# One of the last four row moves of a first DFT given to ScalarE, and a negative mean factor made in one GpSimd step

## The chip, the core and the metric

The kernel runs on one core of a Trainium2 chip. TensorE multiplies matrices, VectorE and ScalarE do elementwise work, GpSimd does elementwise work and issues transfers, SyncE only issues transfers. A transfer (DMA) is carried out by the core's 16 DMA engines, whichever engine issued it. The metric is the device time of one execution in microseconds (us); lower is better. Below, PE is TensorE, DVE is VectorE, ACT is ScalarE, POOL is GpSimd, SP is SyncE, as in the profile.

## The reference, cut to what matters

```python
h = layernorm(x) * (1 + ca) + sa            # x: 4096 rows of 640
X = rfft2(h)                                # over the 4096 rows (the other axis has length 1)
z = X.reshape(..., 4 blocks, 160)
hr, hi = relu2(z @ w1 + b1)                 # complex, block-diagonal
o = softshrink(h @ w2 + b2, 0.01)
x = x + ga * irfft2(o)
h = layernorm(x) * (1 + cb) + sb
x = x + gb * ((silu(h @ w_gate) * (h @ w_up)) @ w_down)
```

`sa, ca, ga, sb, cb, gb` come from `silu(c) @ w_mod`. All of it is float32. The change touches only the first line and the way its result gets into the first part of the transform.

## The kernel before, in words

The 4096 rows are seen as 128 times 32: partition p of a tile holds row p of each of 32 groups, and eight tiles `xa0` to `xa7` hold four groups each (128 partitions by 4 by 640). The first stage handles the eight tiles one after another. For a tile t, `ln_stats(t)` takes mean and variance of each row on DVE (L193, L195) and makes from them, on POOL, the factor `rs` = (variance + eps) to the power -0.5 (L197, L198) and `nm` = -mean * `rs` (L407, L408). `ln_apply(t)` normalises the rows in place: the first rows of a tile on ACT (L419, which needs `rs` and `nm`), the others on DVE (L417, which needs mean and `rs`). How many rows ACT takes is a short table, (4, 2, 2, 3, 2, 3, 2, 1) for the eight tiles. In the first two tiles the statistics are made row by row, in the others four rows at a time. `dft_a(t)` is the first DFT, 128 points over the partitions, on PE (L440), and `evac_a(t)` copies its result from PSUM back into the same tile (L450 on DVE, L452 and L454 on ACT).

The second DFT (`stage_b`, L617) needs the same numbers in another layout: a tile `g` per chunk of frequencies. `moves(t)` brings them there. Most go by way of the DRAM scratch `s1` (`write_s1`, L356, then `load_g`, L312). For chunk 0, which PE wants first, the rows of the tiles 6 and 7 go straight from SBUF to SBUF: `move_g(0, t, i, queue)` (L317) copies the rows of one group i, 16 pieces of 2560 bytes, 40 KB. Each tile has four such moves. In tile 7, i = 0 is issued by POOL and i = 1, 2, 3 by SP, in that order, and PE's first L617 needs all of them. The end of tile 7's evacuation is: i = 0 on ACT, i = 1 on DVE, three weight copies on ACT (L284), i = 2 on ACT (L454), the last columns of all four groups on ACT (L452), i = 3 on DVE (L450).

Behind the moves of tile 7 the queue of SP holds the second half of the weights `w2` (`rr`, L498), more writes of `s1`, and the loads of chunk 1. Behind the last evacuation ACT makes the rounded parts of the weights `w1` and `w2` (L284, L538) and copies a bias (L493), then the first result of the second DFT (`z`, L624). While chunk 0 is on its way PE has matmuls `pz` (L335, 16 passes in the profile) whose result nobody reads.

Everything here is inside `tc.manual_schedule()`: each engine runs its instructions in the order in which the program states them for it. Completion of transfers is counted by eight counters, `DMAHW0` to `DMAHW7`, for those issued by SP and ACT together (POOL has its own). The builder hands the counters out in turn, one transfer after another in its own list; each finished transfer adds 16. A transfer that gets a counter waits first until the transfers that had the counter before it have finished, unless its engine has already waited for that. The waits of an instruction are shown below in brackets.

Of the kernel before, what the change touches and what calls it, by code (L numbers as in the profile page):

```python
# [9 lines left out]
OP = mybir.AluOpType  # L10
# [163 lines left out]
def body(tc, x, w1, b1, w2, b2, wg, wu, wd, c, wm, k_fa, k_tb, k_tx, k_bm, k_bx, k_ga, k_ge, k_id, out, dbg=None):  # L174
    nc = tc.nc
    pe, act, dve, pool = nc.tensor, nc.scalar, nc.vector, nc.gpsimd
# [10 lines left out]
    def layer_stats(pl, src, n, name):  # L187

        st = pl.tile([P, n, 2, 6], F32, tag="st", bufs=3, name=f"st_{name}")
        mv = pl.tile([P, n, 2], F32, tag="mv", bufs=7, name=f"mv_{name}")  # L190
        for i in range(n):
            for h in range(2):
                dve.bn_stats(st[:, i, h, :], src[:, i, h * 320:(h + 1) * 320])  # L193
        for i in range(n):
            dve.bn_aggr(mv[:, i, :], st[:, i, :, :])  # L195
        rs = pl.tile([P, n], F32, tag="rs", bufs=7, name=f"rs_{name}")
        pool.tensor_scalar(rs, mv[:, :, 1], EPS, None, op0=OP.add)  # L197
        pool.tensor_tensor(rs, rs, mhalf[:, :n], op=OP.pow)  # L198
        return mv, rs

    from contextlib import ExitStack
    with ExitStack() as top:
# [9 lines left out]
        mone = per.tile([P, 8], F32, name="mone")  # L212
# [26 lines left out]
        with ExitStack() as af:  # L239
# [11 lines left out]
            def load_weights(pl, w, nm, parts=(0, 1)):  # L251
                raw = [pl.tile([P, 2, NB, BS], F32, tag=tag, name=f"{tag}{nm}") for tag in ("rm", "rr")]
                for i in parts:
                    nc.sync.dma_start(raw[i], w[i])
                return raw
# [41 lines left out]
            def load_tb(ch):  # L297
                tb = lp.tile([P, 4, 128], F32, tag="tb", bufs=2, name=f"tb{ch}")
                nc.sync.dma_start(tb, k_tb[:, 4 * ch:4 * ch + 4])
                tbs[ch] = tb  # L300


            def load_g(ch, us=None):
                if ch not in gs:
                    gs[ch] = fx.tile([P, 4, D], F32, tag="gx", bufs=2, name=f"g{ch}")
                f, e = (ch, 1) if ch < 2 else (2, 2) if ch < 4 else (3, 4)
                src = s1[f].rearrange("(u v) (q e j) d -> e u (v q) (j d)", u=4, e=e, q=4)[ch % e]
                if us is None:
                    nc.sync.dma_start(gs[ch].rearrange("p j d -> p (j d)"), src.rearrange("u r d -> r u d"))
                else:  # L310
                    for u in us:
                        nc.sync.dma_start(gs[ch][u:P:4].rearrange("p j d -> p (j d)"), src[u])  # L312


            def move_g(ch, t, i, dma):
                p = 64 * (t % 2) + 16 * i + t // 2
                dma.dma_start(gs[ch][p:p + 13:4], xas[t][64 * ch:64 * ch + 64:4, i])  # L317
# [23 lines left out]
            with tc.tile_pool(name="sp", bufs=1) as sp:  # L341
# [3 lines left out]
                def load_x(t):  # L345
                    xa = xts[t]
                    if t < 3:
                        for i in range(4):
                            nc.sync.dma_start(xa[:, i, :], xv[:, 4 * t + i, :])
                    else:  # L350
                        nc.sync.dma_start(xa, xv[:, 4 * t:4 * t + 4, :])
                    xas.append(xa)


                def write_s1(t, f):
                    nc.sync.dma_start(s1[f][4 * t:4 * t + 4].rearrange("n r d -> r n d"),  # L356
                                      xas[t][(slice(0, 64, 4), slice(64, P, 4), slice(2, P, 4), slice(1, P, 2))[f]])
# [9 lines left out]
                def moves(t):  # L367
                    if t < 6:
                        write_s1(t, 0)
                    if t < 4:  # L370
                        write_s1(t, 1)
                    if t == 0:
                        load_x(6)
                        nc.sync.dma_start(c5, c)
                    elif t == 1:
                        load_x(7)
                        raws[1] = load_weights(sp, w1, "1")
                    elif t == 2:
                        nc.sync.dma_start(wm1, wm[:, 1])
                    elif t == 3:  # L380
                        load_tb(0)
                        pool.dma_start(b1m, b1[:, 0:8].rearrange("p (r b) -> p r b", r=2))
                        pool.dma_start(b1r, b1[0:64, 8:12])
                        pool.dma_start(b2s[0:1], b2.rearrange("r b o -> (r b o)").unsqueeze(0))
                    elif t == 4:

                        raws[2] = load_weights(rp, w2, "2", (0,))
                        load_g(0, (0, 1))
                    elif t == 5:
                        for f in (2, 3):  # L390
                            write_s1(1, f)
                    elif t == 6:

                        for i in range(4):
                            move_g(0, t, i, (pool, nc.sync)[i // 2])
                        load_g(0, (2,))
                    elif t == 7:
                        for i in range(4):
                            move_g(0, t, i, nc.sync if i else pool)


                def ln_stats(t):
                    n = 1 if t < 2 else 4
                    for i in range(0, 4, n):
                        mv, rs = layer_stats(lp, xas[t][:, i:i + n, :], n, f"a{t}_{i}")
                        nm = lp.tile([P, 4], F32, tag="nm", bufs=7, name=f"nm{t}_{i}")
                        pool.tensor_tensor(nm[:, :n], mv[:, :, 0], rs, op=OP.mult)  # L407
                        pool.tensor_tensor(nm[:, :n], nm[:, :n], mone[:, :n], op=OP.mult)  # L408
                        for k in range(n):
                            stats[t, i + k] = (mv[:, k, 0:1], rs[:, k:k + 1], nm[:, k:k + 1])  # L410

                def ln_apply(t):
                    xa = xas[t]
                    for i in range(4):
                        mean, rs, nm = stats[t, i]
                        if i >= (4, 2, 2, 3, 2, 3, 2, 1)[t]:
                            dve.tensor_scalar(xa[:, i, :], xa[:, i, :], mean, rs, op0=OP.subtract, op1=OP.mult)  # L417
                        else:
                            act.activation(xa[:, i, :], xa[:, i, :], AF.Identity, bias=nm, scale=rs)  # L419
# [23 lines left out]
                def evac_a(t):  # L443
                    xa = xas[t]
                    for i in range(5):
# [7 lines left out]
                        else:  # L453
                            act.activation(xa[:, i, 0:512], pas[t, i], AF.Copy)  # L454

                ln_stats(0)
                ln_stats(1)
                ln_apply(0)
                for t in range(8):
                    if t + 2 < 8:  # L460
                        ln_stats(t + 2)
                    if t + 1 < 8:
                        ln_apply(t + 1)
                    dft_a(t)
                    if t == 6:

                        prep1 = prep_weights(raws[1], w1a, w1b, w1c, True)
                        for job in prep1[:3]:
                            weights_high(*job, pool)
                        first_scale(0, 2)  # L470
                    evac_a(t)
                    if t == 6:
                        first_scale(2, 4)
                    if t == 5:
                        act.activation(sc, c5, AF.Silu)
                    moves(t)
# [625 lines left out]
        with ExitStack() as ff:  # L1102
# [1395 lines left out]
            mv, rs, _ = fst[3]  # L2498
# [103 lines left out]
```

## Time and profile before

| what | value |
|---|---|
| three runs | 1406.67, 1402.82, 1402.7 us; median 1402.82 us |
| the profiled execution | 1405.31 us, of which 1403.5 us are the span that the profile shows |
| PE, DVE, ACT, POOL busy | 98%, 76%, 54%, 43% of the span |
| 40 to 50 us: PE, DVE, ACT, POOL busy | 10.00, 9.38, 8.66, 7.78 us |
| 50 to 54 us: the same | 3.44, 3.90, 3.60, 0.00 us |
| DMA engines, mean busy share, 40 to 50 and 50 to 54 us | 0.94 and 0.71 |
| clock granted to TensorE | 1.00 |

The profiled execution is 2.5 us above the median of the runs, so times inside it are added up against its own 1405.31 us and the difference is carried to the median. A row of the timeline gives start, duration, engine, line, what is written and read, and in brackets how long the engine stood idle before it and what released it; rows with "q" behind the engine's name (SPq, ACTq) are transfers being issued, and their duration is that of the issuing, not of the transfer. The chain of waits goes back from the last instruction to what released it, step by step.

### The profile page before, as it was taken

What the parts mean: (1) busy time and instruction counts of PE and PEld (TensorE: products, weight loads), DVE (VectorE), ACT (ScalarE), POOL (GpSimd) and SP (SyncE); (2) the same over time, 40 slices, a digit from 0 to 9 for tenths busy, and PEclk for the clock granted to TensorE, in tenths of its full rate; (3) what the DMA queues carried; (4) which work ended last, traced back from release to release, by engine and by line L of the source; (5) the groups of instructions that cost most, each with busy time, mean ns of one, the idle gap of its engine ahead of it and who ended that gap; (6) DMA issues with size and microseconds to landing.
All of it is one profiled execution on the core that took longest, in us unless ns stands there. A gap on an engine that the chain in (4) does not pass through costs nothing.

```text
span 1403.5 us, 23813 instructions
## 1 busy us (share of the span) xinstructions
PE 1382.4 (98%) x8418; PEld 1310.8 (93%) x8418; DVE 1063.4 (76%) x1868; ACT 763.5 (54%) x1550; POOL 606.6 (43%) x709
## 2 busy tenths in 40 slices
PE   7999999999999999999999999999999999999998
PEld 2799999968889899899999999999999999999998
DVE  8989888889987888649777767677588757375644
ACT  6889999755554555446455355536163624262341
POOL 5610200167776594335446434547153624042240
PEclk9999999999999999999999999999999999999999
DMA  9975566665998998898867998697998668956534
GB/s 371 335 259 186 184 191 220 202 193 177 324 351 303 338 322 273 314 357 303 314 219 288 379 331 300 220 330 238 372 321 300 230 201 287 349 191 222 196 116 150
DMA packets 170858, 377.34 MB, mean 269 GB/s; under 512 B 22028, under 2 KB 81484, under 8 KB 168724
## 3 DMA queue, kind: packets, MB, share of 16 engines
q1 hardware_dynamic: 161588, 359.31, 74.0%
q0 software_dynamic: 6848, 13.90, 3.1%
q10 hardware_dynamic: 2304, 2.62, 0.5%
q8 instruction: 66, 1.08, 0.3%
q14 instruction: 52, 0.43, 0.1%
HBM read 269.48 MB, written 96.80 MB: 261 GB/s over the span
## 4 chain that ended last, share of the span: by engine, by line
PE 83%; DVE 7%; DMA 4%; POOL 2%; issue 2%; ACT 1%; SPq 0%; ACTq 0%; DVEq 0%; POOLq 0%
PE pw L2112 9%; PE pw L2114 9%; PE pw L2113 9%; PE pc L2414 8%; PE pe L2414 6%; PE pd L2330 6%; PE pc L738 5%; PE pl L681 4%; PE pg L2037 3%; PE pg L2035 3%; PE pg L2036 3%; PE pw L2125 2%; PE pw L2123 2%; PE pw L2124 2%; PE pb L617 2%
## 5 line engine op out<-in xcount | busy, mean ns | idle before, releaser
L1499 DVE TENSOR_TENSOR wb<-r,wb 128x768 fp32r<-128x768 f32 (+3 forms) x170 | 161.0, 957 | 14.3 <-ACT wb L1492 13.9
L2112 PE MATMUL pw<-h,wt 128*128 128x384 f32 x412 | 139.6, 339 | 1.0 <-DMA wt<-td 1.0
L2114 PE MATMUL pw<-h,wt 128*128 128x384 f32 x412 | 138.3, 336 | 0.0
L2113 PE MATMUL pw<-h,wt 128*128 128x384 f32 x412 | 138.1, 335 | 0.0
L1492 ACT ACTIVATE wb<-r 128x768 fp32r<-128x768 f32 (+3 forms) x168 | 104.5, 638 | 54.4 <-PE pw L2125 41.2
L2414 PE MATMUL pc<-wq,L 128*128 128x320 f32 x846 | 132.7, 309 | 0.0
L2173 POOL TENSOR_TENSOR sg<-s_x,sg 128x384 f32<-128x384 f32 x24 | 29.1, 1213 | 234.2 <-DVE s_x L2139 234.2
L2414 PEld LDWEIGHTS pc<-wq,L 128*128 128x128 f32 x846 | 126.3, 188 | 0.0
L2193 DVE TENSOR_TENSOR L<-sg,L 128x384 fp32r<-128x384 f32 x144 | 100.2, 718 | 29.8 <-ACT L L2189 29.3
L2131 ACT ACTIVATE s_x<-pw 128x384 f32<-128x384 f32 x52 | 25.5, 491 | 166.4 <-PE pw L2114 165.8
L2112 PE MATMUL pw<-h,wb 128*128 128x384 f32 x312 | 105.0, 336 | 1.5 <-DVE x L2371 1.5
L2113 PE MATMUL pw<-h,wb 128*128 128x384 f32 x312 | 104.4, 335 | 0.0
L2114 PE MATMUL pw<-h,wb 128*128 128x384 f32 x312 | 104.4, 334 | 0.0
L2414 PE MATMUL pe<-wq,L 128*128 128x320 f32 x648 | 101.8, 309 | 0.4 <-DMA wq<-wqd 0.4
L2035 PE MATMUL pg<-ht,wb 128*128 128x512 f32 x260 | 101.9, 392 | 0.0
L2037 PE MATMUL pg<-ht,wb 128*128 128x512 f32 x260 | 101.4, 390 | 0.1
L2036 PE MATMUL pg<-ht,wb 128*128 128x512 f32 x260 | 101.3, 390 | 0.0
L2184 POOL TENSOR_TENSOR sg<-sg,sg 128x384 f32<-128x384 f32 x72 | 92.5, 1285 | 19.5 <-DVE L L2193 16.0
L2414 PEld LDWEIGHTS pe<-wq,L 128*128 128x128 f32 x648 | 96.5, 188 | 0.7 <-issue 0.7
L2330 PE MATMUL pd<-wq,a 128*128 128x320 f32 x632 | 96.8, 310 | 0.0
L2330 PEld LDWEIGHTS pd<-wq,a 128*128 128x128 f32 x632 | 93.5, 188 | 0.5
L2371 DVE TENSOR_TENSOR x<-x,pe 128x320 f32<-128x320 f32 x108 | 51.7, 483 | 51.1 <-PE pe L2457 31.6
(323 smaller groups left out, 3888.1 us busy)
## 6 DMA issues: line engine op xcount, KB each, us to landing
wq<-wqd SPq DMA_DIRECT2D x83, 640.0 KB, 5.7
wt<-td SPq DMA_DIRECT2D x103, 512.0 KB, 4.5
hs<-ho SPq DMA_DIRECT2D x52, 512.0 KB, 5.8
h<-hs SPq DMA_DIRECT2D x32, 768.0 KB, 8.3
td<-wt SPq DMA_DIRECT2D x25, 512.0 KB, 7.0
r<-in_B_w_gate_dram SPq DMA_DIRECT2D x24, 384.0 KB, 4.6
r<-in_B_w_up_dram SPq DMA_DIRECT2D x24, 384.0 KB, 3.7
xx<-tt SPq DMA_DIRECT2D x56, 160.0 KB, 3.2
```

What stands on the lines that cost most here:

```text
L1492: def high(ks, e=slice(0, c), copy=lambda o, i: act.activation(o, i, AF.Copy)):
L1499: dve.tensor_tensor(wbs[t, n][:, 1, ks, e], raw[t, n][:, ks, e], f32(wbs[t, n][:, 0, ks, e]), op=OP.subtract)
L2035: mm(b, wh, hh, start=(kk == 0), stop=False)
L2036: mm(b, wh, hl, start=False, stop=False)
L2037: mm(b, wl, hh, start=False, stop=(kk == 4))
L2112: mm(b, w(0, kp), a[:, kp, 0], start=start and kp == 0, stop=False, skip_group_check=not start)
L2113: mm(b, w(0, kp), a[:, kp, 1], start=False, stop=False, skip_group_check=not start)
L2114: mm(b, w(1, kp), a[:, kp, 0], start=False, stop=kp == 1, skip_group_check=not start)
L2184: pool.tensor_tensor(o, x, y, op=op)
L2193: dve.tensor_tensor(o[:, 1], raws[j], f32(o[:, 0]), op=OP.subtract)
L2330: mm(b[:, :320], l, m, start=start and i == 0, stop=stop and i == len(s) - 1)
L2414: mm(o[:, :320], ls[q][:, x, k], w[:, q, y], start=start and q == 0 and n == 0, stop=q == 1 and n == 2, skip_group_check=not start)
```

## The change

Two edits in the first stage. In `moves(7)` the group i = 2 is issued by ACT (`nc.scalar`) instead of SP; i = 0 stays on POOL, i = 1 and 3 on SP. In `ln_stats`, for the tiles 0 and 1 (one row at a time), `nm` is made by one POOL instruction with two multiplications, and only for the rows that ACT normalises; for two rows of tile 1, which DVE normalises, it isn't made at all. The other tiles keep their two steps.

```diff
@@ moves @@
                     elif t == 7:
                         for i in range(4):
-                            move_g(0, t, i, nc.sync if i else pool)
+                            move_g(0, t, i, (pool, nc.sync, nc.scalar, nc.sync)[i])
+                ACT_ROWS = (4, 2, 2, 3, 2, 3, 2, 1)
@@ ln_stats @@
-                        pool.tensor_tensor(nm[:, :n], mv[:, :, 0], rs, op=OP.mult)
-                        pool.tensor_tensor(nm[:, :n], nm[:, :n], mone[:, :n], op=OP.mult)
+                        if n > 1:
+                            pool.tensor_tensor(nm[:, :n], mv[:, :, 0], rs, op=OP.mult)
+                            pool.tensor_tensor(nm[:, :n], nm[:, :n], mone[:, :n], op=OP.mult)
+                        elif i < ACT_ROWS[t]:
+                            pool.tensor_scalar(nm[:, 0:1], mv[:, 0, 0:1], rs, -1.0, op0=OP.mult, op1=OP.mult)
@@ ln_apply @@
-                        if i >= (4, 2, 2, 3, 2, 3, 2, 1)[t]:
+                        if i >= ACT_ROWS[t]:
```

On PE, DVE and SP the instructions keep their order, but for the one move that leaves SP; POOL has ten instructions less. The new line numbers are five higher behind the edits.

The first place is SP's queue from the second write of tile 3 (`xa_118`) to the moves of tile 6 (`xa_122`). Here `xa_116` is tile 1, `xa_120` tile 4, `xa_121` tile 5, `s` the scratch, `tb` the table of the second DFT, `rm` and `rr` weights. Before:

```order
L356 DMA s<-xa_118 16x4x640 [waits DMAHW5_49]
L299 DMA tb_408<-in_k_tb_dram 128x512 [waits DMAHW6_49]
L356 DMA s<-xa_120 16x4x640 [waits DMAHW7_49,DVE_49,Activation_49]
L254 DMA rm_453<-in_A_w_dram 128x1280 [waits DMAHW0_49]
L312 DMA g_456<-s 32x2560 [waits DMAHW1_49]
L312 DMA g_456<-s 32x2560 [waits DMAHW4_49,DMAHW2_49]
L356 DMA s<-xa_121 16x4x640 [waits DMAHW3_49,DVE_49,Activation_49]
L356 DMA s<-xa_116 32x4x640
L356 DMA s<-xa_116 64x4x640 [waits DMAHW5_49]
L317 DMA g_456<-xa_122 4x4x640 [waits DMAHW6_49,Activation_49]
L317 DMA g_456<-xa_122 4x4x640 [waits DMAHW7_49,DVE_49]
```

The same place in the changed kernel:

```order
L356 DMA s<-xa_118 16x4x640 [waits DMAHW5_49]
L299 DMA tb_398<-in_k_tb_dram 128x512 [waits DMAHW7_49]
L356 DMA s<-xa_120 16x4x640 [waits DMAHW0_49,DVE_49,Activation_49]
L254 DMA rm_443<-in_A_w_dram 128x1280 [waits DMAHW1_49]
L312 DMA g_446<-s 32x2560 [waits DMAHW2_49]
L312 DMA g_446<-s 32x2560 [waits DMAHW4_49,DMAHW3_49]
L356 DMA s<-xa_121 16x4x640 [waits DVE_49,Activation_49]
L356 DMA s<-xa_116 32x4x640 [waits DMAHW5_49]
L356 DMA s<-xa_116 64x4x640 [waits DMAHW6_49]
L317 DMA g_446<-xa_122 4x4x640 [waits DMAHW7_49,Activation_49]
L317 DMA g_446<-xa_122 4x4x640 [waits DMAHW0_49,DVE_49]
```

No transfer has moved here, but the counters have: `tb` had counter 6 and now has 7, and all behind it are one further on. Counter 6 at that turn has gone to ACT's move, which the builder's list puts between `xa_118` and `tb`. So the holder of counter 6 ahead of the write of tile 1 (`xa_116`, 64x4x640) is now ACT's move of tile 7, and the built program makes that write wait for counter 6 to reach 64: 48 from the three transfers that had it earlier, and 16 from ACT's move.

The second place is SP's queue right behind it, from the load of the third quarter of `g` to the weights `rr`; `xa_123` is tile 7. Before:

```order
L312 DMA g_456<-s 32x2560 [waits DMAHW3_49,DMAHW0_49]
L317 DMA g_456<-xa_123 4x4x640 [waits DMAHW1_49,DVE_49,Activation_49]
L317 DMA g_456<-xa_123 4x4x640 [waits DMAHW2_49]
L317 DMA g_456<-xa_123 4x4x640 [waits DVE_49]
L498 DMA rr_454<-in_A_w_dram 128x1280 [waits DMAHW4_49]
```

And in the changed kernel:

```order
L312 DMA g_446<-s 32x2560 [waits DMAHW4_49,DMAHW1_49]
L317 DMA g_446<-xa_123 4x4x640 [waits DMAHW2_49,DVE_49,Activation_49]
L317 DMA g_446<-xa_123 4x4x640 [waits DMAHW3_49,DVE_49]
L503 DMA rr_444<-in_A_w_dram 128x1280
L356 DMA s<-xa_117 32x4x640 [waits DMAHW5_49]
```

One move of tile 7 has left; with `rr` the counters are in step again.

The third place is ACT behind the last evacuation of tile 7, in the changed kernel:

```order
L459 ACTIVATE xa_123<-pa_2_529 128x512 [waits DVE_49,PE_49]
L457 ACTIVATE xa_123<-pa_4_523 128x4x128 [waits PE_49]
L317 DMA g_446<-xa_123 4x4x640 [waits Activation_49]
L284 ACTIVATE w1a<-rm_311 128x4x128
L284 ACTIVATE w1b<-rm_311 128x4x128
L284 ACTIVATE w1c<-rr_312 128x4x128
```

Before, L284 followed L452 directly; now the move stands between, and waits for ACT's own last evacuation.

## The prediction

> **What bounds the kernel now.** I read the page's chain of waits by engine, then the chain in order of time around the two edited places, then the timelines of PE, SP, ACT and POOL there.
>
> ```profile
> PE 83%; DVE 7%; DMA 4%; POOL 2%; issue 2%; ACT 1%; SPq 0%; ACTq 0%; DVEq 0%; POOLq 0%
> ...
> 38.26 0.33 DVE mv_a L195 x4
> ...
> 49.64 3.39 DMA g<-xa
> 53.03 0.35 issue
> 53.38 2.04 PE pb L617 x16
> ```
>
> Over the whole span PE sets the end. In the first stage it doesn't: from 8.5 to 40 us the chain is DVE's statistics, piece on piece, and then one transfer, a move of tile 7 that SP issues at 49.64 and that lands 3.39 us later, at 53.03. PE starts the second DFT 0.35 us behind it. What PE does around that and afterwards:
>
> ```profile
> 52.10 0.72 PE L335 MATMUL pz<-ones 128*128 128x128 f32 x5
> 53.38 0.57 PE L617 MATMUL pb<-tb,g 128*128 128x128 f32 x3 [0.56 <-DMA g<-xa]
> 54.00:60.00 6.00, 6.00 (x54) 6.00 (x53) 5.09 (x13) 4.83 (x11) 3.77 (x7) 1.00 0.99 303
> 100.00:200.00 100.00, 99.94 (x782) 99.03 (x781) 89.16 (x173) 95.03 (x196) 13.69 (x48) 1.00 0.58 185
> ```
>
> PE stands still for 0.56 us at 53.38 and is then busy without a gap (6.00 of 6.00, 99.94 of 100). So whatever moves the 53.38 moves the end by as much, unless PE's later waits give some back.
>
> **The moves as they are issued.** SP's queue, one row for each issue:
>
> ```profile
> 43.96 0.60 SPq L356 DMA_DIRECT2D s<-xa  x1
> 45.12 0.69 SPq L317 DMA_DIRECT2D g<-xa  x1
> 45.91 1.12 SPq L317 DMA_DIRECT2D g<-xa  x1
> 47.13 0.53 SPq L312 DMA_DIRECT2D g<-s  x1
> 48.43 0.56 SPq L317 DMA_DIRECT2D g<-xa  x1
> 49.04 0.54 SPq L317 DMA_DIRECT2D g<-xa  x1
> 49.64 0.54 SPq L317 DMA_DIRECT2D g<-xa  x1
> 50.22 0.45 SPq L498 DMA_DIRECT2D rr<-in_A_w_dram  x1
> ```
>
> The first is the 640 KB write of tile 1 (64x4x640), then two moves of tile 6, the load of the third quarter of g, the three moves of tile 7, and rr. Read alone, the edit takes out the middle move (49.04) and lets the last one go 0.60 us sooner. But the counters say something else. In the changed kernel the 640 KB write waits for counter 6 at 64, and the last 16 of it come from ACT's move. That move can't be issued before ACT's last evacuation:
>
> ```profile
> 47.81 0.60 ACT L452 ACTIVATE xa<-pa 128x512 f32<-128x512 f32 x1 [0.26 <-PE pa L440]
> 280.43 0.44 ACT L853 ACTIVATE cz<-pi 128x320 f32<-128x320 f32 x1 [0.70 <-PE pi L852]
> 280.89 0.35 ACTq L854 DMA_DIRECT2D s<-cz  x1
> 281.29 0.44 ACT L853 ACTIVATE cz<-pi 128x320 f32<-128x320 f32 x1 [0.42 <-PE pi L797]
> ```
>
> So SP, which now issues the write at 43.96, will stand in front of it until a transfer has landed that starts after 48.41 (47.81 + 0.60). Queued behind the waiting write are both moves of tile 6, the load of g, two moves of tile 7, rr, and all later writes and loads. PE's first L617 needs the five of them that go to g. They are late next.
>
> **Costing it.** That SP really stands still for a landing is seen in the waits of SP's queue; the durations of transfers are in the DMA views (KB each, median us from issue to landing; for the moves, the minimum, median and maximum over all eight).
>
> ```profile
> SPq L312 <- DMA s<-xa: 3.2, 4, 2.2
> ...
> s<-cz ACTq DMA_DIRECT2D x4, 160.0 KB, 1.8
> ...
> s<-xa SPq DMA_DIRECT2D x1, 640.0 KB, 5.4
> ...
> DMA to landing us min/median/max: 3.3/3.9/4.1
> ```
>
> 1. ACT's move is issued at 48.44, by the 0.02 us between the end of L853 (280.43 + 0.44) and the issue at 280.89. An issue of its shape took SP 0.54 to 0.56, the 160 KB on ACT 0.35.
> 2. It lands 1.8 us later (ACT's own transfers, on a quiet queue) or up to 3.9 (median of the moves, with other traffic). By then SP has issued nothing since the write before, at 43.3, and the queues have drained. I take 2.0: landing at 50.45.
> 3. SP wakes. PE's wake-up above was 0.35; I take 0.2: 50.65.
> 4. Six issues in a row, the write, two moves, the load, two moves. All they wait for is long done. The starts of the last five lie 0.60 + 0.56 + 0.56 + 0.53 + 0.56 and five gaps of 0.05 (48.43 + 0.56 to 49.04) behind: 50.65 + 3.06 = 53.7 for the last move. The two long issues before (0.69, 1.12) had older transfers ahead; if they come back, 0.7 more.
> 5. Landing of the last move: 1.8 us if nothing is ahead, 3.39 as now, 4.1 as the slowest. The write of 640 KB, the load and four moves are ahead as before, nothing older is: 2.8, nearer to 3.39. That is 56.5.
> 6. PE starts 0.35 later, at 56.85 instead of 53.38: **+3.5 us**.
>
> With the low ends (1.8, 1.8) it is 53.5 + 1.8 + 0.35 = 55.65, +2.3; with the high ends (3.9, the stalls, 4.1) 56.3 + 4.1 + 0.35 = 60.75, +7.4. The values near the low end are likelier, as the queue is quiet.
>
> *The skill on the wait.* The Trainium skill (DMA: Bandwidth & Descriptors, "Why a DMA increments its semaphore by 16 and not by 1") says that a transfer on k of 16 engines posts 16 - k at once and the rest as each engine's data lands, and that only the full 16 means landed. By that the 64 can't be reached at the issue. If it could, SP would go on at 49.0 and PE at 55.2, +1.8. No row here shows the counter; the 3.2 us of SP's waits for landings agree.
>
> **ACT's side.** The move costs ACT 0.4 to 0.6 us ahead of its weight copies. What covers it:
>
> ```profile
> 53.04 0.56 ACT L538 ACTIVATE w2b<-rm 128x160 fp32r<-128x160 f32 x2
> 54.55 0.69 ACT L624 ACTIVATE z<-pb,ca 128x512 fp32r<-128x512 f32 x1 [0.95 <-PE pb L617]
> ```
>
> ACT has 0.95 us of idle ahead of z, and z itself comes 3.5 later. The last w2b copies reuse tile 1's buffer and wait, before and after, for the 640 KB write; issued at 50.65 and landing after 5.4 at most, that is 56.05, plus 0.56, while z is due at 58.0. Hidden: 0. Without that cover it would be 0.6. rr goes out at 54.3 instead of 50.22, 4.1 later against PE's 3.5, with less ahead of it than its old place had; 0 to 0.6, I take 0.
>
> **POOL's part.** Timeline of the first rows and of the turn to four rows at a time:
>
> ```profile
> 6.54 0.19 POOL L407 TENSOR_TENSOR nm<-mv_a,rs_a 128x1 f32<-128x1 f32 x1
> 6.81 0.19 POOL L408 TENSOR_TENSOR nm<-nm,mone 128x1 f32<-128x1 f32 x1
> 7.07 0.22 POOL L197 TENSOR_SCALAR rs_a<-mv_a 128x1 f32<-128x1 f32 x1
> 17.66 12.06 PE L440 MATMUL pa<-xa,fa 128*128 128x512 f32 x26 [1.58 <-DVE xa L417]
> 17.29 0.41 POOL L197 TENSOR_SCALAR rs_a<-mv_a 128x4 f32<-128x4 f32 x1 [0.60 <-DVE mv_a L195]
> 19.63 1.73 ACT L419 ACTIVATE xa<-xa,nm,rs_a 128x640 f32<-128x640 f32 x2 [2.30 <-POOL nm L408]
> ```
>
> A step less is 0.27 us (6.54 to 6.81), in six rows; two rows lose 0.53 (6.54 to 7.07): 2.7 us of POOL in all. The new instruction isn't in the trace: 0.19 as a product, 0.22 as L197; even at 0.46 it would cost no more than the two it replaces. ACT's rows start up to a microsecond sooner. But PE then waits for DVE (1.58), POOL for DVE (0.60), and ACT for the four rows of the next tile (2.30), all set by DVE's statistics, which don't wait for POOL. The gain ends there: 0. Without that cover, with POOL as the bound to the end of the stage, it would be 2.7.
>
> Sum: 3.5 + 0 + 0. The profiled execution would go from 1405.31 to 1408.8; the runs' median is 2.5 lower, so **1402.8 becomes 1406.3 us**, +0.25%, within the 0.3% (4.2 us) that a measurement of this kernel can tell from no change.
>
> **The rivals.**
>
> *A, PE starts slow again after the gap.* PE would stand from 52.82 (52.10 + 0.72) to 56.85, 4.0 us. The groups of L440 matmuls from 8 to 11 us and from 12 to 15 us:
>
> ```profile
> L440 PE MATMUL pa<-xa,fa 128*128 128x512 f32 x4 | 3.5, 1032 | 8.0 <-ACT xa L419 8.0
> ...
> L440 PE MATMUL pa<-xa,fa 128*128 128x512 f32 x8 | 3.9, 618 | 0.0
> ```
>
> After 8.0 us of idle the first four took 1032 ns each instead of 618; after the 1.58 us at 17.66 the 26 went at 464 ns each (12.06 / 26), at full pace. 4.0 lies between. Price: four times 0.41, 1.7 us, as PE is without a gap behind it: +5.2, 1408.0, slower by 0.37%. Against it: the granted clock reads 1.00 in every stretch, and 4.0 is nearer to 1.58 than to 8.0. It decides as soon as the gap is long enough.
>
> *The skill on this.* The Trainium skill (TensorE: Matmul & The Clock Gate, Part 1: The HAM clock gate) has the array fall to half clock after an idle window of about 3.4 us, in windows that run freely. By that a gap of 4.0 us is cold where it covers a whole window, which it does in some executions only: (4.0 - 3.4) / 3.4, an estimate of one in six. The slow matmuls at 8 us agree.
>
> *B, the counter is slow.* ACT's move lands at 3.9, or the moves behind the 640 KB at 4.1 with the long issues: +5 to +7.4, say 1408.8. For it: the moves' row. Against it: the drained queues.
>
> *C, the wait doesn't bite* (counter 6 reaches 64 otherwise, or early). Then the last move goes 0.60 sooner, and PE can't start before 52.82: at best -0.56, 1402.3. With the early opening, +1.8. Against it: the wait stands in the built program, and nothing else adds to that counter in between.
>
> *D, PE's later waits give some back.* The longest from 300 us on:
>
> ```profile
> PE pw L2112 <- DVE x L2371: 1.5, 1, 1.5
> PE pw L2112 <- DMA wt<-td: 1.0, 1, 1.0
> ```
>
> Only loads that SP issues far ahead could use the time: the 1.0, and a few tenths elsewhere. +2.3, 1405.1.
>
> **How the numbers follow.** Forecast (+2.6 to +4.2 around 3.5) 0.52; A 0.16, as the gap is nearer to the one that cost nothing; B 0.14; C 0.08; D 0.10. A and B are slower by more than 0.3%, and so is a twentieth at the forecast's upper edge: 0.32. C holds what chance there is of faster, 0.02. The rest, 0.66, is within 0.3%. The likeliest gives 1406.3, by itself 1405.4 to 1407.0. The range takes in D and the early opening of C below and A and most of B above: 1403.6 to 1409.0.
>
> **What would show it.** Right: SP issues nothing between 43.9 and about 50.5, then six transfers in three microseconds; PE's wait for a landing before L617 grows from 0.56 to about 4; the DMA engines idle around 49 us; DVE's chain ends at 38.6 as before; ACT's first L419 starts 0.2 sooner. Wrong: SP issues the 640 KB write near 44 (then C); L617's first three matmuls take clearly longer than the 0.57 us of now while the gap is about 4 (A); the 53.38 moves by over 5 us (B); the 53.38 moves by 3.5 and the end by less (D).

## The result and the profile after

The changed kernel takes 1411.5 us (median of 6, 1410.68 to 1413.38) against 1404.15 us of the kernel before (median of 6, 1402.7 to 1406.67). The ratio is 1.0051, with a 95% interval of 1.0041 to 1.0062: 7 us slower, twice what was forecast. Five later runs of it gave 1410.2 us, ratio 1.0043 [1.0031, 1.0055]. The profiled execution has a span of 1410.0 us (before: 1403.5).

SP's queue in the changed kernel (start, duration of the issuing; rows of one kind are drawn together):

```profile
41.24 0.48 SPq L312 DMA_DIRECT2D g<-s  x1
41.94 9.38 SPq L356 DMA_DIRECT2D s<-xa  x3
51.42 1.68 SPq L317 DMA_DIRECT2D g<-xa  x2
```

Three writes that were issued one behind the other before now lie across 9.38 us. The stretch from the third of them on, by itself:

```profile
50.73 0.60 SPq L356 DMA_DIRECT2D s<-xa  x1
51.42 1.68 SPq L317 DMA_DIRECT2D g<-xa  x2
53.20 0.53 SPq L312 DMA_DIRECT2D g<-s  x1
53.82 1.19 SPq L317 DMA_DIRECT2D g<-xa  x2
55.06 0.44 SPq L503 DMA_DIRECT2D rr<-in_A_w_dram  x1
```

The 640 KB write goes out at 50.73 instead of 43.96, and all the rest of the queue stands behind it. ACT at that time:

```profile
47.62 0.60 ACT L457 ACTIVATE xa<-pa 128x512 f32<-128x512 f32 x1 [0.26 <-PE pa L445]
48.24 1.15 ACTq L317 DMA_DIRECT2D g<-xa  x1
...
60.76 0.69 ACT L629 ACTIVATE z<-pb,ca 128x512 fp32r<-128x512 f32 x1 [5.92 <-PE pb L622]
```

ACT issues its move at 48.24, as soon as the last evacuation is through, and SP goes on 2.49 us later. `z` waits 5.92 us for PE, so ACT's own extra work costs nothing. The chain of waits there:

```profile
54.48 3.85 DMA g<-xa
58.33 0.35 issue
58.67 4.74 PE pb L622 x24
```

The last move of tile 7, issued at 54.48, lands 3.85 later. PE begins the second DFT at 58.67, 5.29 later than before (53.38). And the first 24 matmuls take 4.74 us. In the timeline of PE, with the gap ahead of them, and in the windows from 54 to 60 and 60 to 70 us (the last three columns are granted clock, DMA share and GB/s):

```profile
58.67 4.74 PE L622 MATMUL pb<-tb,g 128*128 128x128 f32 x24 [6.05 <-DMA g<-xa]
```

```profile
54.00:60.00 6.00, 1.33 (x6) 1.36 (x7) 0.69 (x4) 0.83 (x4) 0.00 (x0) 0.64 0.83 235
60.00:70.00 10.00, 10.00 (x77) 9.86 (x76) 6.96 (x14) 7.69 (x17) 8.14 (x16) 0.88 0.90 315
```

In the kernel before the row of the same 24 read, at a granted clock of 1.00,

```profile
53.38 2.92 PE L617 MATMUL pb<-tb,g 128*128 128x128 f32 x24 [0.56 <-DMA g<-xa]
```

Now PE has stood for 6.05 us, the clock in that window is 0.64, and 1.82 us more are gone. From matmul to matmul the first 18 start 0.213 us apart, the others 0.111. So PE is about 7.1 us late behind them (5.29 + 1.82).

### The profile page after: what moved, and what is told of

The parts are those of the page before. It is cut to its first block, busy times and chain, and to the rows that moved or that the text cites. A ratio compares the mean times of both kernels' runs of the same rounds, so it can differ in the third digit from the quotient of the medians.

```text
span 1410.0 us, 23805 instructions
## 1 busy us (share of the span) xinstructions
PE 1383.7 (98%) x8418; PEld 1312.7 (93%) x8418; DVE 1063.0 (75%) x1868; ACT 764.6 (54%) x1550; POOL 611.6 (43%) x699
## 4 chain that ended last, share of the span: by engine, by line
PE 85%; DVE 7%; DMA 3%; POOL 2%; ACT 1%; issue 1%; SPq 0%; ACTq 0%; POOLq 0%; DVEq 0%
PE pw L2117 9%; PE pw L2119 9%; PE pw L2118 9%; PE pc L2419 8%; PE pe L2419 6%; PE pc L743 5%; PE pd L2335 4%; PE pl L686 4%; PE pg L2040 3%; PE pg L2042 3%; PE pg L2041 3%; PE pb L622 3%; PE pw L2130 2%; PE pw L2128 2%; PE pw L2129 2%; PE py L1753 1%
## 5 line engine op out<-in xcount | busy, mean ns | idle before, releaser
L1504 DVE TENSOR_TENSOR wb<-r,wb 128x768 fp32r<-128x768 f32 (+3 forms) x170 | 154.7, 920 | 15.7 <-ACT wb L1497 15.4
```

The costliest lines, as they stand in the source:

```text
L1504: dve.tensor_tensor(wbs[t, n][:, 1, ks, e], raw[t, n][:, ks, e], f32(wbs[t, n][:, 0, ks, e]), op=OP.subtract)
```

## The experiments

All times are medians; the kernel before is run beside each.

**Which of the two edits.** First GpSimd's part alone:

```diff
-                            move_g(0, t, i, (pool, nc.sync, nc.scalar, nc.sync)[i])
+                            move_g(0, t, i, nc.sync if i else pool)
```

> Only the GpSimd part of the change: nm in one step for tiles 0 and 1, all three later moves of tile 7 on SP as before. Counter theory (the loss is SP waiting for ScalarE's move): no difference from the kernel before, ratio 0.999 to 1.001, and L617 starts between 53.1 and 53.5 us. Rival (the earlier ScalarE rows and DVE/GpSimd port traffic cost something): 1 to 3 us slower.

1405.18 us, ratio 1.0004 [0.9994, 1.0013]. PE's timeline of this run:

```profile
53.28 2.92 PE L622 MATMUL pb<-tb,g 128*128 128x128 f32 x24
```

The second DFT begins where it did. GpSimd's saved steps don't help, and the new instruction does no harm. Then the move alone, on the kernel before:

```diff
-                            move_g(0, t, i, nc.sync if i else pool)
+                            move_g(0, t, i, (pool, nc.sync, nc.scalar, nc.sync)[i])
```

> Only the move: i = 2 of tile 7 on ScalarE, nm as before. Counter theory: the whole loss, 6.5 to 7.5 us over the kernel before, SP silent from about 43.9 to 50.7, L617 at 58.5 to 59. Rival (both parts needed): clearly less than 6 us.

1411.36 us, ratio 1.0053 [1.0036, 1.007]. SP's queue, then PE:

```profile
42.54 8.85 SPq L356 DMA_DIRECT2D s<-xa  x3
```

```profile
59.17 5.03 PE L617 MATMUL pb<-tb,g 128*128 128x128 f32 x24 [6.46 <-DMA g<-xa]
```

The whole loss belongs to the move.

**Is it the counter, or that ACT carries the row?** All moves stay on SP, as before. ACT issues one more transfer of the same rows at the same place, into a scratch in DRAM that nobody reads:

```diff
+    spare = nc.dram_tensor("spare", (16, D), F32, kind="Internal").ap()
...
+                            if i == 2:
+                                nc.scalar.dma_start(spare, xas[t][0:64:4, i])
```

> The kernel before with all three moves on SP as before, and one more transfer on ScalarE at the same place: the same 16 rows of 2560 bytes, written to a DRAM scratch that nobody reads. It adds 40 KB of work and takes nothing from SP. Counter theory: it takes counter 6 too, SP waits for it in front of the 640 KB write, and the loss is that of the change or 0.6 us more, as SP has seven issues behind the wait instead of six: 7 to 9 us. Rival (the row of g comes late because ScalarE carries it, by a slow queue or late issue): PE doesn't need this transfer, so 0 to 0.6 us.

1410.83 us, ratio 1.0049 [1.0033, 1.0066]. SP's queue, ACT, and PE's first matmuls of the second DFT:

```profile
42.76 8.47 SPq L357 DMA_DIRECT2D s<-xa  x3
...
53.72 1.75 SPq L318 DMA_DIRECT2D g<-xa  x3
```

```profile
48.76 0.58 ACTq L402 DMA_DIRECT2D spare<-xa  x1
```

```profile
59.21 5.46 PE L620 MATMUL pb<-tb,g 128*128 128x128 f32 x24 [6.06 <-DMA g<-xa]
```

Nobody needs ACT's data here, and SP stands as long. What is shared is the counter: by the semaphore events of the trace ACT's transfer lands at 50.61 on the counter for which SP's 640 KB write waits, and the write is issued at 50.63. The rival, that the row comes late because ACT carries it, falls.

**The same move from GpSimd**, whose transfers have counters of their own:

```diff
-                            move_g(0, t, i, (pool, nc.sync, nc.scalar, nc.sync)[i])
+                            move_g(0, t, i, (pool, nc.sync, pool, nc.sync)[i])
```

> The changed kernel with i = 2 of tile 7 issued by GpSimd instead of ScalarE: SP still has one move less, but GpSimd's transfers have counters of their own, so nothing on SP waits for it. Counter theory: the loss is gone; SP's last move goes at 49.0, GpSimd's second at 49.3, landing 3.3 to 3.9 later at 52.6 to 53.2; L617 at 52.8 to 53.5, ratio to before 0.999 to 1.0005. Rival (taking the move off SP is what hurts): clearly slower than before.

1404.73 us, ratio 0.9998 [0.9989, 1.0007]; again, on another chip (e14), 1406.62 us, ratio 1.001 [0.9999, 1.0021]. The loss is gone from the median, and there is no gain. But the runs of e14 reach from 1402.41 to 1411.44 us, those of the kernel before beside them from 1403.6 to 1408.17. In the profiled execution of e6 PE began at 56.06, over 2.5 us behind what was expected, and the chain read

```profile
49.09 0.56 POOL g L317
49.66 6.10 DMA g<-xa
55.76 0.30 issue
```

so one of GpSimd's two moves, issued back to back, landed late. In the profiled execution of e14 it wasn't late, and PE went on without a wait:

```profile
52.52 2.84 PE L622 MATMUL pb<-tb,g 128*128 128x128 f32 x24
```

> The kernel of e6 again, beside the others on one chip: 1403.5 to 1405.5, within 0.1% of the kernel before.

**Another transfer at the counter's next turn.** Tile 1's two writes are put behind the last move of tile 7, ahead of `rr`, so that the next holder of counter 6 is the second move of tile 6:

```diff
-                    elif t == 5:
-                        for f in (2, 3):
-                            write_s1(1, f)
...
+            for f in (2, 3):
+                write_s1(1, f)
             nc.sync.dma_start(raws[2][1], w2[1])
```

> The changed kernel with the two writes of tile 1 (32x4x640 and 64x4x640) put behind the last move of tile 7 on SP instead of ahead of the moves of tile 6. The holder of counter 6 after ScalarE's move is then the second move of tile 6 on SP, eight transfers on in the builder's list. Counter theory: SP stands in front of that move (45.9 before) until about 50.7, has four issues behind the wait instead of six and no 640 KB ahead of them: last issue at 52.5, landing 2.3 to 2.8 later, L617 at 55.3 to 55.7, after a gap under 3 us and so at full pace. ScalarE's w2b copies now wait for those writes, up to 1.2 us more. In all 2 to 3.5 us over the kernel before, 4 to 5 under the changed one. Rival (it is the 640 KB write that waits for ScalarE, for its data): SP doesn't stop ahead of the moves, L617 at 53, no loss there.

1408.36 us, ratio 1.0028 [1.0018, 1.0039], +3.9 us. SP's queue, PE and ACT:

```profile
44.90 6.41 SPq L317 DMA_DIRECT2D g<-xa  x2
51.41 0.51 SPq L312 DMA_DIRECT2D g<-s  x1
52.01 1.20 SPq L317 DMA_DIRECT2D g<-xa  x2
```

```profile
56.53 5.33 PE L621 MATMUL pb<-tb,g 128*128 128x128 f32 x24 [3.93 <-issue]
```

```profile
59.12 0.56 ACT L542 ACTIVATE w2b<-rm 128x160 fp32r<-128x160 f32 x2 [4.84 <-issue]
59.59 0.67 ACT L628 ACTIVATE z<-pb,ca 128x512 fp32r<-128x512 f32 x1
```

The stall has moved with the counter's turn: SP now stands inside the pair of tile 6's moves. With neither the 640 KB write nor its issue in the row, PE starts 2.1 us sooner than in the changed kernel. But a gap of 3.93 us is enough for the slow start (5.33 us for the 24), and the weight copies on ACT now wait 4.84 us for the late writes of tile 1.

**Does TensorE's slow start count?** The matmuls `pz`, which nobody reads, are lengthened, so that the gap ahead of the second DFT shrinks:

```diff
-                idle(8)
+                idle(32)
```

> The changed kernel with 32 instead of 8 of the matmuls whose result nobody reads, so that TensorE is busy to about 57.9 us and stands still for 0.8 instead of 6 us before L617. Clock theory (1.8 us of the loss are matmuls at half pace after the gap): L617's 24 matmuls take 2.7 instead of 4.7 us, the kernel is 1.5 to 2.0 us faster than the changed one and 5 to 5.7 us slower than before. Rival (they were slow for another reason, contention for SBUF with the transfers): still 4 to 4.7 us for the 24, no difference from the changed kernel.

1412.19 us, ratio 1.0058 [1.0043, 1.0073]. PE's timeline, then the longest of its waits behind 300 us:

```profile
50.84 7.39 PE L335 MATMUL pz<-ones 128*128 128x128 f32 x64
59.23 2.92 PE L622 MATMUL pb<-tb,g 128*128 128x128 f32 x24 [1.00 <-DMA g<-xa]
```

```profile
PE py L1753 <- DVE chl L1743: 3.2, 2, 2.3
```

At the spot it does what was expected: no slow start. At the end there is nothing of it. In this profile the slow start came back at another place, behind the second of the waits for `chl`: PE's row, then the stretch from 377.44 to 380.85 us, whose granted clock (third figure from the end) is 0.50:

```profile
377.52 0.64 PE L1753 MATMUL py<-chl,gt 128*128 128x320 f32 x1 [2.29 <-DVE chl L1743]
```

```profile
377.44:380.85 3.41, 3.33 (x10) 2.95 (x11) 3.41 (x6) 2.82 (x6) 3.25 (x4) 0.50 0.96 277
```

Four of the six runs of e4 have a mean granted clock of 0.997 or 0.998, which is what the changed kernel has (0.996 to 0.998). So in most runs of e4 TensorE spent as long at half clock as in the changed kernel, at whatever places.

Shorter settings, `idle(18)` and `idle(12)`, were run once each:

> The changed kernel with 18 instead of 8 of the unread matmuls: the gap before L617 shrinks from 6.0 to about 3.8 us, near the 4.0 of the prediction. If a gap of that length is enough, the 24 matmuls of L617 take 4 us or more; if not, 2.7 to 2.9.

> The changed kernel with 12 of the unread matmuls: a gap of about 5.1 us. The 24 matmuls of L617 take 4 us or more if 5.1 us is enough for the slow pace, 2.7 to 2.9 if not.

Their rows of PE, the first of e7, the second of e8:

```profile
58.73 5.31 PE L622 MATMUL pb<-tb,g 128*128 128x128 f32 x24 [3.94 <-DMA g<-xa]
```

```profile
58.76 5.28 PE L622 MATMUL pb<-tb,g 128*128 128x128 f32 x24 [5.27 <-DMA g<-xa]
```

1412.49 and 1413.07 us, one run each. Gaps of 3.94 and 5.27 us end in a slow start, and so does the 3.93 of e5; gaps of 1.00 (e4) and 2.84 (e6) ahead of the second DFT don't. The changed kernel and e4 were then timed again, beside e5 with `idle(21)`:

> The changed kernel, unchanged, beside the next two on one chip. Both theories: 1410.5 to 1412.5, ratio 1.004 to 1.006.

> The changed kernel with 64 filler matmuls in place of 16, again, with more rounds. Theory A (TensorE's slow start after the gap counts to the end): 1.0 to 2.0 us faster than the changed kernel beside it, so 1409.5 to 1410.5. Rival (what the warm clock saves at 58 us is waited off later, PE then waits for DVE's chl near 350 us): the same as the changed kernel within 1 us, or up to 1 slower.

> The changed kernel with tile 1's two writes behind the last move of tile 7, as in e5, and 42 filler matmuls in place of 16, so that PE idles 1.0 us instead of 3.9 before the second DFT. Theory A: PE starts at 56.5 as in e5, the 24 matmuls take 2.9 us instead of 5.3, and the shift behind them is 3.1 instead of 5.5; at the end 1.5 to 2.4 us faster than e5, 1406 to 1407. Rival (the saving is waited off later): 1408 to 1409, as e5.

1410.2 us (1409.13 to 1411.61), 1410.19 us (1408.13 to 1412.64) and 1410.28 us (1408.06 to 1412.62), ratios 1.0043, 1.0047 and 1.0043. By these ratios neither warm kernel is faster than its cold twin (e10 for e11, e5 for e12). For e12 the profile tells why. PE's timeline:

```profile
56.27 2.92 PE L621 MATMUL pb<-tb,g 128*128 128x128 f32 x24 [0.90 <-issue]
60.24 0.35 PE L685 MATMUL pl<-z,w1a 128*128 128x256 f32 x1 [1.05 <-ACT z L628]
60.94 0.50 PE L685 MATMUL pl<-z,w1a 128*128 128x256 f32 x2 [0.34 <-DVE z L629]
```

Of the 2.4 us that the matmuls save, 1.4 are waited off at once, for `z`, which stands behind ACT's wait for tile 1's late writes; at 71 us e12 is only 0.2 us ahead of e5. For e11 no such wait shows: its profiled execution is 3.4 us shorter than that of e10 (spans of 1406.4 and 1409.8), while its six times fall into two groups, 1408.1 to 1409.0 and 1411.4 to 1412.6. What sends half of them up isn't settled; it isn't the clock, which is 0.999 or 1.000 in both groups. The last of these is the GpSimd kernel without any `pz` (`idle(0)`):

> The kernel of e6 (the move issued by GpSimd) without the 16 filler matmuls, so that TensorE idles 4.9 us instead of 2.84 ahead of the second DFT, and nothing else is late. Local: the 24 matmuls take 5.3 us instead of 2.92. Theory A (the slow start counts to the end): 1.8 to 2.4 us more than the kernel of e6 beside it, 1406 to 1407. Rival (it is absorbed later): the same as e6 within 0.8 us.

1407.03 us, ratio 1.0009 [1.0001, 1.0018], against 1406.62 of e14 beside it. PE's row:

```profile
54.40 4.54 PE L622 MATMUL pb<-tb,g 128*128 128x128 f32 x24 [3.17 <-DMA g<-xa]
```

The slow start is there, 1.6 us of it, and no difference at the end that can be told from the scatter, since PE's start in this kernel varies by more (52.52, 54.40 and 56.06 in the three profiles, with the landing of GpSimd's moves). So this pair doesn't decide it either.

**How much of a delay reaches the end?** For this the kernel before was profiled once more, and then PE alone was delayed in it, by longer `pz`.

> The kernel before, unchanged, for a second profile of it. Question: how far do two executions of one kernel drift apart along PE's matmuls? In every other profile the distance to the first profile of before shrinks by about 1.2 us between 290 and 310 us and by another 1.2 between 1000 and 1100. If those are peculiarities of that one execution, this profile shows the same two steps, both of about -1.2, and ends 1 to 2.5 us shorter than it began. If they are a true give-back of the later kernels' delay, this profile lies within 0.3 us of the first at all places.

1403.41 us, span 1401.6. How much later the matmuls start than in the first profile of before, in us, at places given by their time in that profile (worked out from the start times of both traces):

```
                      71    275    315    500   1000   1100   1390
before, again      -0.50  -0.11  -1.74  -0.26  -0.06  -1.26  -1.93
changed            +6.80  +6.87  +6.57  +6.81  +6.94  +5.60  +6.50
changed, again     +8.24  +8.25  +6.72  +8.18  +8.20  +6.86  +6.32
e5                 +5.37  +5.59  +3.95  +4.78  +4.85  +3.52  +2.98
e11                +6.17  +6.50  +5.91  +5.04  +4.21  +2.91  +2.86
```

The two steps down, between 275 and 315 (mostly made up again by 500) and between 1000 and 1100, are in the repetition of before too: they belong to the first profile, not to the change. The two executions of one kernel end 1.93 us apart. Against the repetition, the changed kernel is 7.3 us late at 71 and between 6.9 and 8.4 from there to the end, and its second execution 8.7 and then 8.1 to 8.5: what was lost at the start stays lost. e5 and e11 lose 1.0 and 1.9 us of their distance on the way, which is no more than two executions of one kernel drift.

```diff
-                idle(8)
+                idle(32)
```

> The kernel before with 64 filler matmuls instead of 16: no transfer moves, the clock stays up, and TensorE begins the second DFT when the fillers end, at 52.82 + 48 x 0.112 = 58.2, 4.8 us later than now. If every microsecond of delay at this place reaches the end: +4.8 us, ratio 1.0034. If later waits take some of it (rival D): +1.5 to +3.5.

> The kernel before with 40 filler matmuls instead of 16: the fillers end at 55.5, the second DFT begins 2.1 us later. If every microsecond reaches the end: +2.1, ratio 1.0015. If later waits take it, as the 2.7 us of e6 seem to have been taken: 0 to +0.7, ratio below 1.0005.

1412.51 us, ratio 1.0055 [1.0043, 1.0067], and with `idle(20)` 1408.04 us, ratio 1.0026 [1.0016, 1.0036]. PE's rows in e15, its longest later wait, and PE in e16:

```profile
51.52 7.39 PE L335 MATMUL pz<-ones 128*128 128x128 f32 x64
58.75 2.84 PE L617 MATMUL pb<-tb,g 128*128 128x128 f32 x24
```

```profile
PE py L1748 <- DVE chl L1738: 3.3, 2, 2.4
```

```profile
55.24 2.84 PE L617 MATMUL pb<-tb,g 128*128 128x128 f32 x24
```

A delay of 5.4 us at the spot (53.38 to 58.75) costs 6.0 to 9.4 at the end, one of 1.9 costs 2.2 to 5.1. In sum nothing is absorbed; if anything more is lost. The row on `chl` shows one place where: PE waits there 3.3 us in e15, 2.6 in e16, 3.2 in e4, 2.1 in e7 and 2.6 in e8, all with longer `pz`, but not in e11 and e12, and 0 to 1.2 in the profiles with 16 passes of `pz` or none. Why longer `pz` should bring it, 300 us behind, stays open. It also blurs what e4 says of the slow start, and what e15 and e16 say of the delay: without the 2.9 and 2.2 us by which this wait is longer than in the first profile of before (0.4), 3.1 to 6.5 and 0 to 2.9 us would be left, so these two by themselves don't exclude that a part is given back.

## Why the prediction was wrong

What failed is the size of the steps 4 and 5 (3.06 and 2.8 us forecast, 3.75 and 3.85 measured), and that TensorE's slow start was kept out of the sum, as a rival with a chance of 0.16, where it cost 1.82 us.

**The mechanism was right.** SP stands in front of the 640 KB write until ACT's move has landed, six transfers follow in a row, and PE's first L622 waits for the last; e3 shows that the counter alone does it. The DMA engines were idle as foreseen (a share of 0.00 from 48.20 to 49.40 us). Rival C, that the wait doesn't bite, is out. GpSimd's part was costed at 0 and is (e1). ACT's side was costed at 0 and is, as `z` waits for PE. `rr` too: POOL's copies come 5.5 us later, and PE never waits for them.

**The terms of the sum were too small**, in the profiled execution:

| step | forecast | measured |
|---|---|---|
| 1, ACT's move issued | 48.44 | 48.24 |
| 2 and 3, landing and wake-up | 2.0 + 0.2 | 2.49 together |
| 4, from the write to the last move | 3.06 | 3.75 (50.73 to 54.48) |
| 5, landing of the last move | 2.8 | 3.85 |
| 6, PE's start behind it | 0.35 | 0.34 |
| PE's start | 56.85 | 58.67 |

The differences, -0.20, +0.29, +0.69, +1.05 and -0.01, give the 1.82 by which PE starts later than forecast (that the slow start costs the same figure is chance). The largest is step 5. The forecast took 2.8 because nothing older was ahead of the moves; but with the 640 KB write, the load and three other moves issued in the 3.75 us before, it was 3.85 here, and 4.27 and 4.44 in the chains of e2 and e10, near the slowest move of before (4.1). With the write out of the way (e5) the move before the last took 3.34, and the last, issued at 52.66, landed at 56.12, 3.46 later: so the write alone doesn't explain the miss. In step 4 the long issues, which were noted as "0.7 more" and left out, came back: the two moves behind the 640 KB write took 0.69 and 0.88 to issue instead of 0.56 each, and the five gaps 0.49 together instead of 0.25. In step 2 the issue itself was slow, 1.15 us on ACT for what takes SP 0.54; the move landed at 50.71, and SP went on 0.02 later, not 0.2.

**Rival A came on top**, and was weighed wrongly. It was given 0.16, because a gap of 4.0 us was "nearer to the one that cost nothing". The gap became 6.05. But even the forecast's own gap would have done: 3.93 (e5) and 3.94 (e7) both ended in a slow start, 2.84 (e6) did not. With the mechanism right and only the sizes as forecast, A was the likelier case, as far as two executions tell. Its price was put at 1.7, as four slow matmuls; it is 1.82 here, over 18 of them, and 2.4 to 2.5 where nearly all 24 are slow (e5, e3), so that the 1.7 came close in part by luck. The granted clock of 1.00 in all stretches, which stood against it, could not speak on this: in the stretches shown, PE had no such gap.

The traces of the experiments show how the clock falls. The granted clock is 1.00 or 0.50, and each stretch at 0.50, but for the one at the end of a profile, lasts 3.41 us or twice that. Here are the 3.41 us ahead of such a stretch, and the stretch itself, for the changed kernel, for e5, and for e1, where PE stood 2.12 us at 69.75, waiting for DVE (behind the window's length: PE's busy time; third figure from the end: the granted clock):

```profile
52.25:55.66 3.41, 0.38 (x4) 0.18 (x2) 2.44 (x7) 2.58 (x10) 0.00 (x0) 1.00 0.82 255
55.66:62.49 6.83, 3.82 (x18) 3.85 (x19) 0.75 (x1) 0.71 (x2) 0.73 (x2) 0.50 0.92 308
```

```profile
51.36:54.77 3.41, 1.24 (x12) 1.05 (x10) 3.30 (x10) 2.91 (x11) 0.00 (x0) 1.00 0.43 135
54.77:61.59 6.82, 5.06 (x24) 5.09 (x25) 1.04 (x2) 2.07 (x5) 0.00 (x0) 0.50 1.01 335
```

```profile
69.18:72.59 3.41, 1.29 (x11) 1.10 (x9) 1.27 (x4) 1.50 (x3) 3.41 (x7) 1.00 1.04 410
72.59:76.00 3.41, 3.41 (x15) 3.36 (x15) 3.33 (x8) 0.42 (x1) 3.41 (x7) 0.50 1.03 401
```

In the 3.41 us ahead of the fall PE was busy for as much as 1.29 us, so it need not have been idle throughout: a gap of little over 2 us was enough in e1 and e4 (2.12 and 2.29), while 2.84 in e6 and 2.4 in e15 passed without a fall. That this hangs on how a gap lies to windows of 3.41 us fits all of these, but the windows aren't in the traces where the clock doesn't fall. The Trainium skill (TensorE: Matmul & The Clock Gate, Part 1: The HAM clock gate) puts the fall of the clock behind an idle window of about 3.4 us. The length agrees with the 3.41 here; read as a window that is idle throughout, the rule does not. The prediction's estimate of one in six for 4.0 us counted only gaps that cover a whole window; two slow starts in two don't bear it out.

**Rival B** had half of it: the landings behind the 640 KB came near its 4.1 and the long issues were there, while ACT's own landing was 2.5 and not 3.9. Its sign, that the 53.38 moves by over 5 us, came (5.29); its 1408.8 lacked A. **Rival D** falls for this kernel: against the repetition of before, the distance doesn't shrink in either profile of the changed kernel, and the shrinking against the first profile, which looks like it, is also there between two executions of one kernel.

So the forecast of +3.5 became +5.29 at PE's start and +7.1 behind its first matmuls, and +7.2 at the end. That the two together reach the end is shown by the medians and by the two profiles of the changed kernel. That the slow start by itself does is likely from these, but not shown apart: the runs made for it (e4, e11 to e13) did not show it.

## What to carry to other kernels

Before a transfer is given to another queue, look up which completion counter it takes and which transfer has that counter next: if that one stands ahead of things that are needed sooner, its whole queue waits for the new transfer to land, however idle the engine that took it over. Where transfers have been held back by such a wait, cost them at the slow end of what the profile shows for them, since they all go out at once. And when a delay opens a gap on TensorE, compare the gap with the shortest one that is known to end in a slow start (2.12 us here), not with the longest that cost nothing, and where it is clearly longer (3.9 us and more here) add the price to the likeliest case and not to a rival.

## What the runs showed that was not expected

- The same 40 KB move takes SP 0.54 us to issue (0.69 to 1.12 behind long transfers) and ACT 1.15 (48.24), while ACT's transfer of the same rows to DRAM took 0.58 (e3, with other pieces at the far end).
- TensorE's slow start ahead of the second DFT: none behind gaps of 0.90 (e12), 1.00 (e4), 1.06 (e11) and 2.84 us (e6); one behind 3.17 (e13), 3.93, 3.94, 5.27, 6.05, 6.06, 6.46 and 6.64 us (e10). At other places 2.12 and 2.29 us were enough. PE works at half clock for 3.4 us (e13) to 5.6 us (e3, beyond the 24 matmuls), at 0.213 us from matmul to matmul instead of 0.111. The Trainium skill (same page and part) gives, for bf16, N over 1.2 GHz for a cold matmul, 0.107 us for 128 columns; the 0.213 of these float32 matmuls is twice that, and the ratio of cold to warm, 1.9, agrees with its half clock.
- Two of GpSimd's moves, issued back to back, can land as late as 6.1 us behind the issue of the last (e6), or so early that PE doesn't wait (e14), in the same kernel.
- Two executions of one kernel drift apart by up to 1.9 us and back along the way, so a distance at one place of two profiles is no measure of what an edit costs at the end.
